# Sliding-window attention feeding a two-layer MLP on one core: one transpose instead of two for a unit's two key blocks, split again by masks

## The chip, the cores and the metric

The kernel runs on one NeuronCore of a Trainium2 chip, in one launch. The metric is the device time of a run in microseconds (us), as the median of its runs. Five engines matter: TensorE (PE in the profile, with its weight loads as PEld), VectorE (DVE), ScalarE (ACT), GpSimd (POOL) and SyncE (SP), which here issues every DMA. Each engine works through its own list of instructions in order; they meet through semaphores.

## What is computed

Four batches of eight heads of attention over 768 positions with head size 64, then a two-layer MLP over all 3072 tokens:

```python
scores = (q @ k.T) / sqrt(64)
keep   = (key < n_sink) | ((0 <= query - key) & (query - key < window))   # n_sink 4, window 128
a      = softmax(where(keep, scores, -1e9));  attn = a @ v
x      = attn with the heads side by side       # (4*768, 512)
r      = maximum(x @ w_in, 0)                   # w_in 512 x 2048
out    = (s * r * r + b) @ w_out                # w_out 2048 x 512
```

With a window of 128 a query block of 128 sees at most two key blocks: its own (keys not after the query) and the one before (keys less than 128 back). In the block before, the kept keys have a place in the block greater than the query's place; in its own block, not greater. The two kept triangles, laid on each other, don't overlap. The sink keys stand in 16 columns of their own.

## The kernel before, in words

The 3072 tokens are cut into eight chunks of 384 (three query blocks; two chunks a batch). Chunk 0 has a way of its own (`first_slots`), during which the MLP's weights are also loaded and converted. From then on `moe_steps` of chunk c is interleaved with `attn_slots` of chunk c+1. The MLP has 32 steps: for each of 16 slices of the hidden layer, L521 (12 matmuls, the first layer) and, two slices later, L540 (9 matmuls, the second). The last chunk's MLP has no attention beside it.

Precision is kept by splitting values in two: a rounded part (hi, type fp32r) and the rest (lo), which are multiplied apart.

An attention chunk has 24 units, one for each head and query block (h, i), and runs as a software pipeline, one slot at a time. In slot t it issues `unit_a` of unit t, `unit_b` of unit t-LB, `unit_c` of unit t-LC and `unit_d` of unit t-LC-LD; before the change LB, LC, LD are 2, 4, 1, so there are 29 slots, spread evenly over the 32 MLP steps.

- `unit_a`: two score matmuls (PE L293, L294), mask and row maximum (DVE L298), exponential with its row sum (ACT L304) into the tile `sm` (four buffers), and on POOL a copy of the sink columns into `psk` (L305).
- `unit_b`: one PE transpose for each key block of the exponentials: L316 for the block before, L317 for its own, both into the PSUM tile `tp`. Then hi is rounded out of `tp` by ACT (L321) and lo is what is left, by DVE (L322). The two parts go to `hl`. Where a unit has no block before it (first block of a sequence, in even chunks), there is no L316.
- `unit_c`: the value matmuls (PE L354) with `vv`, which hold hi and lo of the values; at the head's third block ACT (L362) and DVE (L363) gather the sum into `xm`; once a pair of heads, transposes of `psk` (L367) and two copies.
- `unit_d`: once a pair of heads, sink values and the scale 1/sum (L378, L380), two DVE operations on `xm` (L381, L382), then hi (ACT L383) and lo (POOL L384) of the MLP's input x.

Ahead of them `prep_head` splits queries (L268, L272), keys (ACT L271, POOL L273) and values (ACT L277, POOL L278), two slots before a head's first unit. SP issues the loads: queries L235, values L237, keys L250 (one raw buffer each), sink values L257.

The code is written against tiles. A scheduler orders the instructions of each engine ahead of time; the order of the program is their priority, and an instruction that opens a tile waits until a buffer of that tag is free. Nothing is reordered on the chip. PSUM has five buffers of tag `a` (scores, `tp`, the first layer's `h`, `o`, `os`, `zb`, `ts`) and three for the second layer's sums.

In the MLP, L521 gives `h`; ACT L524, DVE L526, ACT L528 and DVE L529 turn it into `g`, which L540 reads two slices later (three buffers of `g`).

Of the kernel before, what the change touches and what calls it, by code (L numbers as in the profile page):

```python
# [6 lines left out]
F32 = mybir.dt.float32  # L7
# [5 lines left out]
ALU = mybir.AluOpType  # L13
AX = mybir.AxisListType

P = 128
# [3 lines left out]
CH = BLK * P  # L20
# [6 lines left out]
MDT = mybir.dt.bfloat16  # L27
# [4 lines left out]
NARROW, NEARLY = 2, 8  # L32
RB, VB = 2, 2
E0, LB0, LC0 = 8, 4, 6
LB, LC, LD, L2 = 2, 4, 1, 2


@with_exitstack
def tile_kernel(ctx, tc, qT, kT, k0, v, vsk, n_sink, window, w, s, b, out):
    nc = tc.nc  # L40
# [21 lines left out]
    nw = const.tile([P, 2], F32, tag="nw", name="nw")  # L62
    n_ap, w_ap = nw[:, 0:1], nw[:, 1:2]
    W = 2 * P + NS
    msk = const.tile([P, 3 * W + P + NS], MDT, tag="msk", name="msk")
    m_1, m_odd, m_even = (msk[:, j * W:(j + 1) * W] for j in range(3))
    m_0 = msk[:, 3 * W:]
# [62 lines left out]
    def constants2():  # L130

        spread = wk.tile([P, P], F32, tag="y", name="spread", bufs=1)
        nc.gpsimd.memset(spread, 0.0)
        for j in range(2):
            nc.gpsimd.affine_select(
                out=spread[96:P].rearrange("p (a d) -> p a d", a=2), in_=spread[96:P].rearrange("p (a d) -> p a d", a=2),
                pattern=[[1, 2], [0, D]], compare_op=ALU.not_equal, fill=1.0, base=2 * j, channel_multiplier=-1)
        nc.scalar.copy(sel, spread)
        for t in psks:
            nc.gpsimd.memset(t, 0.0)  # L140

        nc.vector.tensor_tensor(out=tmp[:, :NS], in0=low[:, :NS], in1=snk[:, :NS], op=ALU.mult)
        nc.vector.tensor_tensor(out=tmp[:, :NS], in0=snk[:, :NS], in1=tmp[:, :NS], op=ALU.subtract)
        nc.vector.scalar_tensor_tensor(out=tm2[:, :NS], in0=rel1[:, :NS], scalar=w_ap, in1=snk[:, :NS],
                                       op0=ALU.is_ge, op1=ALU.mult)
        mask(m_0[:, :NS], tmp[:, :NS])
        mask(m_1[:, 2 * P:], tm2[:, :NS])
        mask(m_even[:, P:P + NS], snk[:, :NS])
        cp = nc.gpsimd.tensor_copy
        upm, lom = m_full[2][:, P:2 * P], m_full[2][:, 2 * P:]  # L150
        cp(out=m_0[:, NS:], in_=lom)
        for m, l0 in ((m_1, P), (m_even, P + NS), (m_odd, P)):
            cp(out=m[:, :P], in_=upm)
            cp(out=m[:, l0:l0 + P], in_=lom)
        cp(out=m_odd[:, 2 * P:], in_=m_even[:, P:P + NS])
# [125 lines left out]
    def unit_a(k, h, i):  # L281

        hd = k.heads[h]
        pp = k.pairs[h // 2]
        g = k.half * BLK + i
        u = (k.c * H + h) * BLK + i
        if k.half == 0:
            c0, n = ((0, 144), (16, 272), (144, 272))[i]
        else:
            c0, n = ((0, 272), (128, 272), (272, 272))[i]  # L290
        sc = ps("sc")
        qs = slice(i * P, (i + 1) * P)
        nc.tensor.matmul(sc[:, :n], hd.qs[:, qs], hd.kh[:, c0:c0 + n], start=True, stop=False)  # L293
        nc.tensor.matmul(sc[:, :n], hd.qs[:, qs], hd.kl[:, c0:c0 + n], start=False, stop=True)  # L294
        m = m_0 if g == 0 else m_1 if g == 1 else m_odd if g % 2 else m_even
        uu = slice(u, u + 1)
        sm = wk.tile([P, W], F32, name="sm", tag="sm", bufs=SMB)
        nc.vector.tensor_tensor_reduce(out=sm[:, :n], in0=sc[:, :n], in1=m, scale=-0.125, scalar=BIG,  # L298
                                       op0=ALU.add, op1=ALU.min, accum_out=negm[:, uu])

        k.cc[(h, i)] = (sm,) + ((NS, None, 0) if g == 0 else (P, 0, 2 * P) if g % 2 else (P + NS, 0, P))
        s0 = k.cc[(h, i)][3]
        hh = h % 2
        nc.scalar.activation(sm[:, :n], sm[:, :n], AF.Exp, bias=negm[:, uu], scale=-1.0, accum_out=pp.zz[:, i, hh:hh + 1])  # L304
        nc.gpsimd.tensor_copy(out=pp.psk[:, i, :6 * NS].rearrange("p (t x) -> p t x", t=3)[:, :, hh * NS:(hh + 1) * NS],  # L305
                              in_=sm[:, s0:s0 + NS].unsqueeze(1).to_broadcast([P, 3, NS]))

    def unit_b(k, h, i):

        sm, c0, p0, _ = k.cc.pop((h, i))  # L310
        hd = k.heads[h]
        if i == 0:
            hd.hl = wk.tile([P, 2, 2 * CH], F32R, name="hl", tag="hl", bufs=HLB)
        tp = ps("tp")
        if p0 is not None:
            nc.tensor.transpose(tp[:, :P], sm[:, p0:p0 + P], ident)  # L316
        nc.tensor.transpose(tp[:, P:2 * P], sm[:, c0:c0 + P], ident)  # L317

        a, z = (P if p0 is None else 0), 2 * P
        hi, lo = (hd.hl[:, t, i * z + a:(i + 1) * z] for t in range(2))  # L320
        nc.scalar.copy(hi, tp[:, a:z])  # L321
        nc.vector.tensor_tensor(out=lo, in0=tp[:, a:z], in1=hi.bitcast(F32), op=ALU.subtract)  # L322
        pp = k.pairs[h // 2]
        if h % 2 == 1 and i == BLK - 1:
            zr = wk.tile([P, 2, BLK, 2], F32, tag="zr", name="zr")
            zh = wk.tile([P, BLK, 2], F32R, tag="zh", name="zh")
            nc.vector.tensor_scalar(out=zr[:, 0], in0=pp.zz, scalar1=1e-9, scalar2=None, op0=ALU.add)
            nc.vector.reciprocal(out=zr[:, 1], in_=zr[:, 0])
            nc.vector.tensor_copy(zh, zr[:, 1])
            nc.gpsimd.tensor_copy(out=pp.psk[:, :, 96:98], in_=zh.bitcast(F32))  # L330
            nc.vector.tensor_tensor(out=pp.psk[:, :, 98:100], in0=zr[:, 1], in1=zh.bitcast(F32), op=ALU.subtract)

    def unit_c(k, h, i):

        hd = k.heads[h]
        pp = k.pairs[h // 2]
        cur = i if k.half == 0 else i + 1
        if i == 1:
            hd.o = ps("o")
            hd.n = 0  # L340

        mm = []
        if i == BLK - 1:
            mm.append((cur, 2 * i + 1, 1))
        if i > 0:
            mm.append((cur - 1, 2 * i - 1, 2))
        if i == 1 and k.half == 1:
            mm.append((0, 0, 1))  # L350
        for kb, c0, n in mm:
            for t in range(2):
                q0 = c0 // 2 * P
                nc.tensor.matmul(hd.o[:, q0:q0 + n * P], hd.vv[:, kb, :], hd.hl[:, t, c0 * P:(c0 + n) * P],  # L354
                                 start=(hd.n == 0), stop=(i == BLK - 1 and kb == cur - 1 and t == 1))
                hd.n += 1
        if i == BLK - 1:
            a, c = (0, D) if h % 2 == 0 else (D, 0)
            if h % 2 == 0:
                pp.x = wk.tile([P, CH], F32, tag="xm", name="xm")  # L360
                pp.y = wk.tile([P, CH], F32, tag="y", name="y", bufs=1)
            nc.scalar.copy(pp.y[a:a + D], hd.o[c:c + D, :CH])  # L362
            nc.vector.tensor_tensor(out=pp.x[a:a + D], in0=hd.o[a:a + D, :CH], in1=pp.y[a:a + D], op=ALU.add)  # L363
            if h % 2 == 1:
                ts = ps("ts")
                for j in range(BLK):
                    nc.tensor.transpose(ts[:, j * P:(j + 1) * P], pp.psk[:, j, :], ident)  # L367
                pp.xs = wk.tile([P, CH], F32R, tag="xsk", name="xsk", bufs=1)
                nc.scalar.copy(pp.xs, ts[:, :CH])
                nc.vector.tensor_tensor(out=pp.xs[32:64], in0=ts[32:64, :CH], in1=pp.xs[32:64].bitcast(F32), op=ALU.subtract)  # L370
# [15 lines left out]
    def attn_slots(c):  # L386
        k = new_chunk(c)
        units, ahead = [], {}
        for pr in range(H // 2):
            h, t0 = 2 * pr, 2 * BLK * pr  # L390
            units += [(h + hh, i) for hh in range(2) for i in range(BLK)]
            todo = ((-5, load_pair, pr), (-5, load_keys, h), (-2, load_sinks, pr), (-2, prep_head, h), (-2, load_keys, h + 1),
                    (1, prep_head, h + 1))
            for d, fn, a in todo:
                ahead.setdefault(max(t0 + d, 0), []).append((fn, a))
        n = len(units)

        def slot(t):
            def f():

                for fn, a in ahead.get(t, ()):
                    fn(k, a)
                if t < n:
                    unit_a(k, *units[t])
                if 0 <= t - LB < n:
                    unit_b(k, *units[t - LB])
                if 0 <= t - LC < n:
                    unit_c(k, *units[t - LC])
                if 0 <= t - LC - LD < n:
                    unit_d(k, *units[t - LC - LD])  # L410
            return f

        return k, [slot(t) for t in range(n + LC + LD)]


    def first_slots():
# [271 lines left out]
    for c in range(NC_):  # L688
# [4 lines left out]
        i = 0  # L693
# [57 lines left out]
```

## Time and profile before

| what | value |
|---|---|
| median of 3 runs | 783.11 us (782.27 to 783.18) |
| profiled execution, own time | 784.06 us |
| its span, first to last instruction | 782.2 us, so 1.9 us lie around it |
| mean granted TensorE clock | 0.983 |
| MLP of chunks 1, 3, 5 (attention of 2, 4, 6 beside it) | 86.47 us each |
| MLP of chunks 2, 4, 6 (attention of 3, 5, 7 beside it) | 89.40 to 89.43 us each |
| MLP of chunk 7, alone | 74.42 us |

How to read it: a row of the profile names the line of the code, the engine, what is written and read, the shape and the count. "Busy" is time in which the engine worked; matmuls overlap each other, so a matmul's duration is longer than the time that it takes from the next one, which is read from the distance between two starts. The time before the MLP of chunk 1 (to 180.09 us) holds the start-up, chunk 0, chunk 1's attention and the weights.

### The profile page before, as it was taken

Reading aid. Unit: us, or ns where it says so; the run is one execution under the profiler, and the core shown is the slowest. Engines: PE = TensorE matmul, PEld = TensorE weight load, DVE = VectorE, ACT = ScalarE, POOL = GpSimd, SP = SyncE. Lnnn points to the kernel's source line nnn. Section 1 sums busy time; section 2 is a strip of 40 time slices with the busy share of each in tenths; the row PEclk is TensorE's granted clock in tenths of the full one; section 3 lists DMA queues with packets and bytes.
Section 4 is the critical chain, followed back from the end, with each engine's and each line's share of the span. In section 5 each row is a group of like instructions: output and inputs, shape, how many; then the busy total and the mean of one; then the engine's idle time right before and its main releaser. Section 6 shows DMA issues by size and latency. Waiting matters only on the chain.

```text
span 782.2 us, 12150 instructions
## 1 busy us (share of the span) xinstructions
PE 736.0 (94%) x4036; PEld 656.5 (84%) x4036; DVE 510.5 (65%) x1251; ACT 495.0 (63%) x1231; POOL 263.4 (34%) x411
## 2 busy tenths in 40 slices
PE   6878887599999999999999999999999999999996
PEld 3656675489989999999989999999989999999985
DVE  5888899985676466665676466665676466653321
ACT  4896977766676576656676576656676576643222
POOL 3146567652333234232333234232333234210000
PEclk9998999989999999999999999999999999999999
DMA  7644304212111211112111211112111211001001
GB/s 275 268 148 176 111 14 160 85 34 75 43 44 53 85 47 52 49 43 76 43 43 53 86 47 53 49 43 76 43 43 53 85 47 53 28 1 41 1 1 44
DMA packets 28118, 54.21 MB, mean 69 GB/s; under 512 B 3600, under 2 KB 16528, under 8 KB 26128
## 3 DMA queue, kind: packets, MB, share of 16 engines
q1 hardware_dynamic: 28048, 53.36, 20.8%
q8 instruction: 34, 0.56, 0.3%
q14 instruction: 36, 0.29, 0.1%
HBM read 47.06 MB, written 6.29 MB: 68 GB/s over the span
## 4 chain that ended last, share of the span: by engine, by line
PE 77%; DVE 7%; ACT 6%; POOL 4%; issue 3%; DMA 1%; SPq 1%; POOLq 0%; DVEq 0%; ACTq 0%
PE h L521 31%; PE po L540 30%; PE o L354 5%; PE sc L294 2%; PE sc L293 2%; POOL w L203 2%; PE tp L317 2%; PE tp L316 2%; DVE w L201 1%; ACT w L199 1%; DVE wt L200 1%; PE o L480 1%; DMA sb<-in_s 1%; ACT sm L304 1%; ACT w L208 1%
## 5 line engine op out<-in xcount | busy, mean ns | idle before, releaser
L521 PE MATMUL h<-x,w 128*128 128x384 f32 x1536 | 301.1, 345 | 13.3 <-DVE r L526 7.2
L540 PE MATMUL po<-w,g 128*128 128x512 f32 x1152 | 298.5, 401 | 4.9 <-DVE g L529 3.7
L521 PEld LDWEIGHTS h<-x,w 128*128 128x128 f32 x1536 | 270.8, 191 | 21.4 <-issue 5.4
L540 PEld LDWEIGHTS po<-w,g 128*128 128x128 f32 x1152 | 209.4, 189 | 46.3 <-DVE g L529 5.5
L524 ACT ACTIVATE r<-h 128x384 f32<-128x384 f32 x128 | 62.8, 491 | 110.2 <-PE h L521 103.2
L298 DVE CUSTOM_DVE_ANT_0 sm<-sc,msk 128x272 f32<-128x272 f32 (+1 forms) x168 | 70.2, 418 | 82.4 <-PE sc L294 60.6
L529 DVE SCALAR_TENSOR_TENSOR g<-r,sb,g 128x384 fp32r<-128x384 f32 x128 | 87.2, 681 | 44.7 <-ACT g L528 42.6
L526 DVE SCALAR_TENSOR_TENSOR r<-h,sb,r 128x384 f32<-128x384 f32 x128 | 78.5, 613 | 52.7 <-ACT r L524 52.5
L305 POOL COPY psk<-sm 128x48 f32<-128x48 f32 x168 | 51.8, 309 | 168.4 <-ACT sm L304 167.3
L304 ACT ACTIVATE sm<-sm,negm 128x272 f32<-128x272 f32 (+1 forms) x168 | 85.3, 508 | 22.2 <-DVE negm L298 21.5
L528 ACT ACTIVATE g<-r,sb 128x384 fp32r<-128x384 f32 x128 | 78.8, 615 | 29.3 <-DVE r L526 29.0
L273 POOL TENSOR_TENSOR kl<-kraw,kh 128x544 fp32r<-128x544 f32 (+1 forms) x56 | 71.9, 1283 | 56.4 <-ACT kh L271 54.2
L321 ACT CAST hl<-tp 128x256 fp32r<-128x256 f32 (+1 forms) x168 | 59.1, 353 | 27.2 <-PE tp L317 26.6
L354 PE MATMUL o<-hl,vv 128*128 128x256 f32 (+1 forms) x400 | 71.6, 295 | 1.8 <-DVE hl L322 0.9
L322 DVE TENSOR_TENSOR hl<-tp,hl 128x256 fp32r<-128x256 f32 (+1 forms) x168 | 66.6, 398 | 8.0 <-ACT hl L321 6.1
L278 POOL TENSOR_TENSOR vv<-vraw,vv 128x256 fp32r<-128x256 f32 (+1 forms) x56 | 42.5, 758 | 60.7 <-ACT vv L277 58.7
L354 PEld LDWEIGHTS o<-hl,vv 128*128 128x128 f32 x400 | 55.0, 190 | 4.1 <-issue 1.4
L363 DVE TENSOR_TENSOR xm<-o,y 64x384 f32<-64x384 f32 x56 | 30.9, 552 | 31.5 <-ACT y L362 31.3
L294 PE MATMUL sc<-kl,qs 128*128 128x272 f32 (+1 forms) x168 | 48.7, 290 | 0.4 <-POOL kl L273 0.4
L293 PE MATMUL sc<-kh,qs 128*128 128x272 f32 (+1 forms) x168 | 47.9, 285 | 0.7 <-DVE qs L272 0.4
L272 DVE TENSOR_TENSOR qs<-qraw,qs 64x384 fp32r<-64x384 f32 x56 | 42.4, 758 | 6.2 <-ACT qs L268 4.5
L317 PE MATMUL tp<-identr,sm 128*128 128x128 f32 x168 | 46.0, 274 | 0.0
(113 smaller groups left out, 837.6 us busy)
## 6 DMA issues: line engine op xcount, KB each, us to landing
w<-in_w SPq DMA_DIRECT2D x15, 1024.0 KB, 10.0
kraw<-in_kT SPq DMA_DIRECT2D x32, 272.0 KB, 2.6
out<-ot SPq DMA_DIRECT2D x24, 256.0 KB, 2.0
qraw<-in_qT SPq DMA_DIRECT2D x28, 192.0 KB, 2.3
kraw<-in_kT SPq DMA_DIRECT2D x24, 208.0 KB, 2.4
vraw<-in_v SPq DMA_DIRECT2D x16, 256.0 KB, 2.6
vraw<-in_v SPq DMA_DIRECT2D x12, 192.0 KB, 2.3
vsraw<-in_vsk SPq DMA_DIRECT2D x28, 64.0 KB, 1.8
```

What stands on the lines that cost most here:

```text
L273: nc.gpsimd.tensor_tensor(out=hd.kl[:, :kw], in0=hd.k[:, :kw], in1=hd.kh[:, :kw].bitcast(F32), op=ALU.subtract)
L293: nc.tensor.matmul(sc[:, :n], hd.qs[:, qs], hd.kh[:, c0:c0 + n], start=True, stop=False)
L294: nc.tensor.matmul(sc[:, :n], hd.qs[:, qs], hd.kl[:, c0:c0 + n], start=False, stop=True)
L298: nc.vector.tensor_tensor_reduce(out=sm[:, :n], in0=sc[:, :n], in1=m, scale=-0.125, scalar=BIG, op0=ALU.add, op1=ALU.min, accum_out=negm[: ...
L304: nc.scalar.activation(sm[:, :n], sm[:, :n], AF.Exp, bias=negm[:, uu], scale=-1.0, accum_out=pp.zz[:, i, hh:hh + 1])
L322: nc.vector.tensor_tensor(out=lo, in0=tp[:, a:z], in1=hi.bitcast(F32), op=ALU.subtract)
L354: nc.tensor.matmul(hd.o[:, q0:q0 + n * P], hd.vv[:, kb, :], hd.hl[:, t, c0 * P:(c0 + n) * P], start=(hd.n == 0), stop=(i == BLK - 1 and kb ...
L521: nc.tensor.matmul(h[:, :CH], weight[f][:, 0, wi, cc * P:(cc + 1) * P], x[xi][:, cc, :], start=(i == 0), stop=(i == 11))
L526: nc.vector.scalar_tensor_tensor(out=r, in0=h[:, :CH], scalar=sw_ap, in1=r, op0=ALU.mult, op1=ALU.mult)
L528: nc.scalar.activation(gg[:, 0, :], r, AF.Identity, bias=b_ap, scale=1.0)
L529: nc.vector.scalar_tensor_tensor(out=gg[:, 1, :], in0=r, scalar=b_ap, in1=gg[:, 0, :].bitcast(F32), op0=ALU.add, op1=ALU.subtract)
L540: nc.tensor.matmul(po[tb], gg[:, gi, tsl], weight[f][:, 1, wi, :], start=(f == 0 and i == 0), stop=(f == NF - 1 and i == 2))
```

## The change

From the third attention chunk on (`k.c >= MERGED`, MERGED = 2), for every unit that has a block before it:

- right after the exponential, POOL adds the two key blocks of `sm`, 128x128 each, into the place of the unit's own block;
- `unit_b` transposes that sum alone (L316 is not issued);
- DVE multiplies the transposed sum by two masks (`split`, 128 x 2 x 128 in bf16, built once by two DVE operations in `constants2`) and writes a 128x256 tile `two` in SBUF, which has one buffer: first the block before, then the own block;
- ACT rounds hi out of `two` instead of `tp`, and lo is computed on POOL, from `two`, instead of on DVE from `tp`.

For these chunks LB goes from 2 to 3 and LC from 4 to 6, so that there are 31 slots. `xm` goes from two buffers to one. `sm` keeps its four buffers, and the values' `vv` its two.

```diff
-LB, LC, LD, L2 = 2, 4, 1, 2
+LB, LC, LD, L2 = (2, 3), (4, 6), 1, 2
+MERGED = 2
...
+    split = const.tile([P, 2, P], MDT, tag="split", name="split")
...
+        nc.vector.tensor_scalar(out=split[:, 0, :], in0=rel, scalar1=0.0, scalar2=None, op0=ALU.is_gt)
+        nc.vector.tensor_scalar(out=split[:, 1, :], in0=rel, scalar1=0.0, scalar2=None, op0=ALU.is_le)
...
+        if g > 0 and k.c >= MERGED:
+            c1, p1 = k.cc[(h, i)][1:3]
+            nc.gpsimd.tensor_tensor(out=sm[:, c1:c1 + P], in0=sm[:, p1:p1 + P], in1=sm[:, c1:c1 + P], op=ALU.add)
...
-        if p0 is not None:
+        merged = p0 is not None and k.c >= MERGED
+        if p0 is not None and not merged:
             nc.tensor.transpose(tp[:, :P], sm[:, p0:p0 + P], ident)
         nc.tensor.transpose(tp[:, P:2 * P], sm[:, c0:c0 + P], ident)
...
-        nc.scalar.copy(hi, tp[:, a:z])
-        nc.vector.tensor_tensor(out=lo, in0=tp[:, a:z], in1=hi.bitcast(F32), op=ALU.subtract)
+        if merged:
+            two = wk.tile([P, 2 * P], F32, tag="two", name="two", bufs=1)
+            nc.vector.tensor_tensor(out=two.rearrange("p (s c) -> p s c", s=2), in0=tp[:, P:2 * P].unsqueeze(1).to_broadcast([P, 2, P]),
+                                    in1=split, op=ALU.mult)
+            nc.scalar.copy(hi, two)
+            nc.gpsimd.tensor_tensor(out=lo, in0=two, in1=hi.bitcast(F32), op=ALU.subtract)
+        else:
+            nc.scalar.copy(hi, tp[:, a:z])
+            nc.vector.tensor_tensor(out=lo, in0=tp[:, a:z], in1=hi.bitcast(F32), op=ALU.subtract)
...
-                pp.x = wk.tile([P, CH], F32, tag="xm", name="xm")
+                pp.x = wk.tile([P, CH], F32, tag="xm", name="xm", bufs=1)
...
+        lb, lc = LB[c >= MERGED], LC[c >= MERGED]
...
-                if 0 <= t - LB < n:
-                    unit_b(k, *units[t - LB])
+                if 0 <= t - lb < n:
+                    unit_b(k, *units[t - lb])
...
-        return k, [slot(t) for t in range(n + LC + LD)]
+        return k, [slot(t) for t in range(n + lc + LD)]
```

(The calls of `unit_c` and `unit_d` take `lc` in the same way.)

## Rows read from the trace of the kernel before

**Rows 1.** The page's table of engines (busy us, share of the span, instructions), and the granted TensorE clock in 40 slices of the span, in tenths.
```profile
PE 736.0 (94%) x4036; PEld 656.5 (84%) x4036; DVE 510.5 (65%) x1251; ACT 495.0 (63%) x1231; POOL 263.4 (34%) x411
PEclk9998999989999999999999999999999999999999
```

**Rows 2.** Busy time of each engine by stretch. Each stretch runs from the first L521 matmul of one chunk's MLP to the next one's; columns: stretch, its length, busy us (and instructions) of each engine, granted clock, DMA share, GB/s. The first six are the MLPs of chunks 1 to 6 with the attention of chunks 2 to 7 beside them, the seventh is the MLP of chunk 7.
```profile
180.09:266.56 86.47, 85.98 (x493) 79.19 (x492) 55.39 (x148) 55.92 (x152) 28.11 (x53) 1.00 0.18 55
266.56:355.96 89.40, 89.08 (x517) 82.28 (x516) 57.64 (x148) 58.37 (x152) 29.38 (x53) 1.00 0.18 55
355.96:442.44 86.48, 85.99 (x493) 79.21 (x492) 55.40 (x148) 56.04 (x152) 27.75 (x53) 1.00 0.18 55
442.44:531.87 89.43, 89.11 (x518) 82.31 (x517) 57.58 (x148) 58.32 (x152) 29.39 (x53) 1.00 0.18 55
531.87:618.34 86.47, 85.98 (x493) 79.20 (x492) 55.36 (x148) 56.13 (x152) 27.76 (x53) 1.00 0.18 55
618.34:707.77 89.43, 89.11 (x518) 82.31 (x517) 57.06 (x150) 55.97 (x146) 25.37 (x49) 1.00 0.13 39
707.77:782.19 74.42, 67.90 (x339) 60.78 (x337) 19.94 (x33) 20.43 (x37) 0.89 (x1) 0.98 0.06 23
```

**Rows 3.** Timeline of PE, two places of the fifth attention chunk; columns: start us, duration us, what, count (instructions of one kind in a row are merged).
```profile
384.67 2.27 PE L540 MATMUL po<-w,g 128*128 128x512 f32 x9
386.78 0.29 PE L293 MATMUL sc<-kh,qs 128*128 128x272 f32 x1
...
395.39 0.29 PE L293 MATMUL sc<-kh,qs 128*128 128x272 f32 x1
395.51 0.29 PE L294 MATMUL sc<-kl,qs 128*128 128x272 f32 x1
395.64 0.27 PE L316 MATMUL tp<-identr,sm 128*128 128x128 f32 x1
395.75 0.27 PE L317 MATMUL tp<-identr,sm 128*128 128x128 f32 x1
395.78 2.35 PE L540 MATMUL po<-w,g 128*128 128x512 f32 x9
397.96 0.29 PE L293 MATMUL sc<-kh,qs 128*128 128x272 f32 x1
```

**Rows 4.** Groups of instructions by line and shape from 180 to 708 us: count, busy us, mean ns of one, idle time of the engine just before them and what ended it.
```profile
L316 PE MATMUL tp<-identr,sm 128*128 128x128 f32 x120 | 32.9, 274 | 0.0
L322 DVE TENSOR_TENSOR hl<-tp,hl 128x256 fp32r<-128x256 f32 x120 | 50.1, 417 | 7.6 <-ACT hl L321 6.1
L321 ACT CAST hl<-tp 128x256 fp32r<-128x256 f32 x120 | 44.3, 370 | 26.9 <-PE tp L317 26.4
L277 ACT CAST vv<-vraw 128x256 fp32r<-128x256 f32 x24 | 9.4, 393 | 0.0
L260 POOL TENSOR_TENSOR vs<-vsraw,vs 32x128 fp32r<-32x128 f32 x24 | 10.9, 455 | 53.6 <-issue 39.7 <-ACT vs L259 13.6
L278 POOL TENSOR_TENSOR vv<-vraw,vv 128x192 fp32r<-128x192 f32 x22 | 14.7, 667 | 29.7 <-ACT vv L277 29.3
L278 POOL TENSOR_TENSOR vv<-vraw,vv 128x256 fp32r<-128x256 f32 x24 | 18.1, 754 | 22.8 <-ACT vv L277 21.1
L305 POOL COPY psk<-sm 128x48 f32<-128x48 f32 x144 | 38.8, 269 | 161.2 <-ACT sm L304 160.3
L384 POOL TENSOR_TENSOR x<-xm,x 128x384 fp32r<-128x384 f32 x25 | 25.3, 1012 | 39.5 <-ACT x L383 39.5
L273 POOL TENSOR_TENSOR kl<-kraw,kh 128x544 fp32r<-128x544 f32 x24 | 32.6, 1357 | 29.2 <-ACT kh L271 28.0 <-PE tp L317 1.2
L273 POOL TENSOR_TENSOR kl<-kraw,kh 128x416 fp32r<-128x416 f32 x22 | 23.9, 1088 | 21.6 <-ACT kh L271 21.2 <-PE tp L317 0.3
```

**Rows 5.** The same view over the whole execution: the mask operations of the start-up on a 128x128 tile with a bf16 result.
```profile
L98 DVE TENSOR_SCALAR m_all<-sc 128x128 bf16<-128x128 f32 x6 | 0.9, 221 | 0.0
```

**Rows 6.** One line's instructions from 180 to 708 us: count, duration in ns (smallest, median, largest), first and last start, shape. L529 and L272 read two tiles in SBUF; L526 reads one in PSUM and one in SBUF.
```profile
L272 DVE TENSOR_TENSOR qs<-qraw,qs x46: 551/552/1031, 189.0 to 673.2; 64x384 fp32r<-64x384 f32 x46
L529 DVE SCALAR_TENSOR_TENSOR g<-r,sb,g x96: 599/619/687, 184.2 to 702.0; 128x384 fp32r<-128x384 f32 x96
L526 DVE SCALAR_TENSOR_TENSOR r<-h,sb,r x96: 601/614/621, 182.9 to 700.7; 128x384 f32<-128x384 f32 x96
L305 POOL COPY psk<-sm x144: 216/223/562, 183.5 to 693.9; 128x48 f32<-128x48 f32 x144
```

**Rows 7.** Timeline of ACT, DVE and POOL in the fourth attention chunk: start us, duration us, what; in brackets the engine's idle time before it and what ended that.
```profile
300.70 0.51 ACT L383 CAST x<-xm 128x384 fp32r<-128x384 f32 x1 [0.56 <-DVE xm L382]
301.30 1.01 POOL L384 TENSOR_TENSOR x<-xm,x 128x384 fp32r<-128x384 f32 x1 [0.79 <-ACT x L383]
...
303.17 0.35 ACT L321 CAST hl<-tp 128x256 fp32r<-128x256 f32 x1
303.55 0.42 DVE L322 TENSOR_TENSOR hl<-tp,hl 128x256 fp32r<-128x256 f32 x1
```

**Rows 8.** What SP's queue waited for, whole execution: us in total, times, longest us.
```profile
SPq L250 <- POOL kl L273: 168.8, 30, 14.9
SPq L237 <- POOL vv L278: 83.6, 23, 9.2
```

More of the change, by code (lines that the diff above doesn't have):

```diff
@@ L404, in f @@
                     unit_a(k, *units[t])
-                if 0 <= t - LB < n:
-                    unit_b(k, *units[t - LB])
[L407 to L410, printed above, removed]
+                if 0 <= t - lb < n:
+                    unit_b(k, *units[t - lb])
+                if 0 <= t - lc < n:
+                    unit_c(k, *units[t - lc])
+                if 0 <= t - lc - LD < n:
+                    unit_d(k, *units[t - lc - LD])
             return f
-        return k, [slot(t) for t in range(n + LC + LD)]
+        return k, [slot(t) for t in range(n + lc + LD)]
     def first_slots():
```

## The prediction

> **What bounds the kernel now.** I read the table of engines first. PE is busy for 736.0 of the 782.2 us of the span, DVE for 510.5, ACT for 495.0, POOL for only 263.4, and the granted clock is near full speed almost throughout [rows 1]. A share of the span is a mean over unlike stretches, so the second view is busy time by chunk. The reader is to see that from 180 us on PE leaves 0.49 us idle in a stretch of 86.47 us and 0.32 us in one of 89.40, at a granted clock of 1.00, while DVE and ACT each idle for about 31 us and POOL for about 60 [rows 2]. The six stretches are the ones in which attention chunks 2 to 7 run, just those that the change touches. Here time is what PE has to issue, and an instruction taken from PE is worth what it takes of PE's sequence.
>
> That is not its duration, since matmuls overlap. The third view, PE's timeline, gives the distances: a score matmul starts at 395.39, the first transpose at 395.64, the second at 395.75, so the first takes 0.11 us [rows 3]. A second way: from 395.39 to the next unit's score matmul at 397.96 are 2.57 us, with nine L540 in them, and nine L540 alone take 386.78 - 384.67 = 2.11; of the remaining 0.46 the two score matmuls take 395.64 - 395.39 = 0.25, which leaves 0.21 for two transposes, 0.105 each [rows 3]. The 274 ns of the group's row [rows 4] would be two and a half times too much.
>
> **The change part by part.**
> PE, removed: chunks 3, 5, 7 have 24 units with a block before, chunks 2, 4, 6 have 16, so 3 x 24 + 3 x 16 = 120 of L316, which is the count of the row [rows 4]. Between 0.105 and 0.11 I take 0.108: 120 x 0.108 = 13.0 us (12.6 to 13.2), 2.6 for an odd attention chunk and 1.7 for an even one. No PE work is added. The transpose that stays reads the sum instead of one block: the same shape, the same time.
>
> POOL, added: an add of 128 elements a partition and a subtract of 256. The subtract has its row, 754 ns at 256 elements; the add lies between 455 ns (128 elements on 32 partitions) and 667 (192 elements on 128), and I take the first, since that is its length in each partition [rows 4]. Together 1.21 us a unit, 29.0 for an odd chunk and 19.3 for an even one, which brings POOL from 29.4 to 58.4 us of 86.8, and from 28 to 47 of 84.8 [rows 2]. It stays beside PE, at nothing, as long as its queue keeps pace.
>
> DVE: the subtract (417 ns, one PSUM and one SBUF input) goes, a multiply of the same shape with one PSUM and one SBUF input comes; I take 417 for it too [rows 4], so nothing. Its bf16 mask, and the PSUM tile read twice, have no row; I bound it by 221 ns, the operation with a bf16 tile on 128 columns [rows 5], and 614, L526 on 384 [rows 6]: 24 units x 0.2 make 5 us a chunk either way, against 31 idle. ACT: the copy reads SBUF, 393 ns instead of 370 [rows 4], 24 x 0.023 = 0.6 us a chunk, hidden by ACT's 31 idle us. If these covers were gone, the two would cost at most their own 5.6 us a chunk.
>
> Start-up: two mask operations at 221 ns [rows 5], 0.4 us on DVE before 180 us, where PE does wait for others; I take all 0.4, bounds 0 and 0.4.
>
> The new order in the queues. Before, DVE waited for ACT; now ACT waits for DVE, POOL for ACT, and, because `two` has one buffer, the next unit's DVE multiply for POOL's subtract. Behind that multiply in DVE's list stand L298, L526 and L529, and PE's next scores, `h` buffers and second layer wait for those. The loop is 0.42 + 0.39 + 0.75 [rows 4] plus three handoffs of 0.03 to 0.09 [rows 7], 1.75 us, and a slot of an odd chunk has 86.8 / 31 = 2.80. About 1.05 us is left for what stands ahead in ACT's and POOL's lists. A key split of 1357 ns comes once a head, so one unit in three [rows 4]. It can overrun by 0.3 alone, by 0.8 with an ACT operation of 0.5 ahead too; DVE has a third of its time idle to catch up. The POOL add stands in front of the transpose, but units now wait three slots instead of two, 8.4 us, for the chain mask, exponential, add.
>
> SP: no DMA is added or moved. But the values' buffers come free at slot +8 after a head's first unit instead of +6 (`unit_c` moved), so the POOL split of the next values, and the load L237 that waits for it (83.6 us of waits), come about two slots later, with key loads L250 behind it in the same list; L250 itself already waits 168.8 us for POOL's key splits [rows 8]. Keys are split two slots, 5.6 us, ahead of their scores; that hides it, and I cost it at nothing. Without that cover each of 48 heads would wait for a key split, up to 1.36 us, which makes 65 us; I keep to nothing, since the values that came late are themselves used only seven slots after a head's first scores, and leave the other end outside the range with the worst of the cases below. `xm` with one buffer: L384, 1.01 us [rows 4], reads it last, two slots before the next pair writes; nothing.
>
> Stalls that PE gets from all this: none is the lower end. PE idles 3 x 0.49 + 3 x 0.32 = 2.4 us in the six stretches today [rows 2]. With POOL's load doubled I take another 2 us.
>
> DVE and POOL in each other's way: L272 takes 552 ns in the median and up to 1031, POOL's sink copy 223 and up to 562; L526, with one input in PSUM, never leaves 601 to 621 [rows 6]. With POOL twice as busy, 16 L529 and 8 L272 a chunk may each be held for part of a 0.75 us subtract, at most 24 x 0.75 = 18 us on DVE, whose 58 would become 76 of 86.8: still not the bound. The Trainium skill (SBUF — State Buffer, "Who interferes with whom") has the same rule: a VectorE instruction with two SBUF inputs and a GpSimd one that reads SBUF keep each other out for a whole instruction, one with a single SBUF input does not. By it the moved subtract meets L529 and L272, and the new multiply meets nothing; the sum would stay, and case (a) below gains weight.
>
> **The sum.** Against the profiled execution: 784.06 - 13.0 + 0.4 + 2.0 = 773.5. The median of the runs is 0.95 lower than that execution, so 772.5 as a median, 1.4% less.
>
> **The rivals.**
> (a) *Part of the gain goes into the loop around `two`.* For: the loop's 1.75 us with a key split and an ACT operation ahead is 3.6 against 2.8. If nothing hid the overrun, 8 heads x 0.8 = 6.4 us an odd chunk and, with a split of 1.09 on shorter keys [rows 4], about 5 an even one: 34 us. Against: DVE's 31 idle us and the second layer's two slices of lead hide most. A quarter coming through is 8.5: 784.06 - 13.0 + 0.4 + 8.5 - 0.95 = 779.
> (b) *Slower: POOL becomes the pace.* Its list is in order. Today it waits 160.3 us for the exponentials before 144 sink copies, 1.11 each [rows 4], at no cost. If it kept all these waits, 24 x 1.11 = 26.7 in a chunk, and waited for ACT's copy before each subtract too (0.48, 11.6), an odd chunk would take 58.4 + 26.7 + 11.6 = 96.7, 7.3 over today's 89.4, while an even one with 47.2 + 26.7 + 7.7 = 81.6 stays under PE. 784.06 + 3 x 7.3 - 3 x 1.7 + 0.4 - 0.95 = 800. It decides from 89.4 - 58.4 = 31.0 us of waits on, 1.29 a unit. For: two more in-order waits on one engine, and a single buffer that hands its delay to DVE. Against: a POOL that lags finds its inputs ready, so the waits shrink just when it gets late; the three slots between stages let it lag.
> (c) *The change does nothing on PE.* Excluded by the count: 120 matmuls and weight loads are not issued, and PE's stretches have no idle time in which they could have been free.
>
> **How the numbers follow.** A measurement of this kernel tells about 0.2% (1.6 us) from no change. Forecast 0.62; (a) 0.18, of which 0.13 ends faster and 0.05 within 0.2%; (b) 0.20. I give (b) that much because the order of the lists was fixed ahead of time and I can't see it. So faster 0.75, same 0.05, slower 0.20. The forecast's own range is 769 (13.2 saved, no stall, part of today's idle time gone) to 776; the range goes on through (a) and the first part of (b), to 786.
>
> **What would show it.** Right: L316 falls from 144 to 24; the six stretches shorten by about 2.4 and 1.5 us with PE still under 1 us idle in each; POOL rises to about 58 and 47 us, L322's group to 48 with the multiply at about 417 ns beside it; `sm`'s sum and the subtract near 0.46 and 0.75. Wrong: PE idle of several us in a stretch, ended by DVE L298, L526 or L529, or by POOL's add ahead of the transpose; DVE's multiply waiting for POOL's subtract; odd chunks that lose more than even ones, as (b) says; new operations well over their rows.

## The result and the profile after

The changed kernel takes 792.26 us (median of 4 runs, 791.73 to 792.89) against 783.14 for the kernel before beside it: a ratio of 1.0112, interval 1.0098 to 1.0125. It is slower by 1.1%; forecast was 772.5, in a range of 769 to 786.

The span of the profiled execution is 790.2 us, 8.0 more than before. Busy time by chunk, cut as in [rows 2] at the first L537 matmul of each chunk's MLP (lines have shifted: L537 is the old L521, L556 the old L540):

```profile
178.94:267.29 88.35, 84.77 (x478) 77.47 (x476) 58.23 (x148) 56.30 (x152) 47.45 (x85) 1.00 0.18 54
267.29:358.21 90.92, 86.95 (x493) 79.60 (x492) 62.93 (x148) 58.76 (x152) 58.33 (x101) 1.00 0.18 54
358.21:446.57 88.36, 84.78 (x477) 77.44 (x476) 58.30 (x148) 56.37 (x152) 46.97 (x85) 1.00 0.18 54
446.57:537.51 90.94, 87.03 (x494) 79.65 (x492) 62.68 (x148) 58.49 (x152) 58.40 (x101) 1.00 0.18 54
537.51:625.86 88.35, 84.75 (x477) 77.44 (x476) 58.40 (x148) 56.33 (x152) 46.96 (x85) 1.00 0.18 54
625.86:715.60 89.74, 86.97 (x494) 79.60 (x493) 60.15 (x150) 56.63 (x146) 54.56 (x97) 1.00 0.13 39
```

The six stretches last 536.66 us against 527.68 [rows 2]. PE is busy for 515.25 of them instead of 525.25, so the work did leave PE; but it idles for 21.4 us instead of 2.4. POOL stands at 47 and 58 us, as worked out, and has over 31 us idle in every stretch. The granted clock is 1.00 as before. The first stretch begins 1.15 us earlier than before, so the start-up lost nothing.

Who ended PE's idle time, from the view of waits between 179 and 716 us (engine, line, by whom; us in total, times, longest), and two waits of the new path:

```profile
PE os L393 <- DVE xsk L385: 21.4, 18, 1.3
POOL hl L334 <- ACT hl L333: 18.3, 34, 1.9
DVE two L331 <- POOL hl L334: 2.6, 11, 0.3
```

The one wait of PE is that of the sink values' matmul `os` (`unit_d`) for DVE's last step on the sink tile `xsk` (`unit_c`, one slot earlier). It comes 18 times, at three of the four pairs of each chunk; 17 of the waits last 1.2 to 1.3 us, the last one 0.2. Before, the same wait held 2.4 us in six times. The loop around `two`, of which I had feared most, is 2.6 us.

The groups of the new path, 179 to 716 us, to be held against [rows 4], and the query split L276, the old L272, whose row before is in [rows 6]:

```profile
L331 DVE TENSOR_TENSOR two<-tp,split 128x256 f32<-128x256 f32 x120 | 50.2, 418 | 16.4 <-PE tp L325 12.9 <-POOL hl L334 2.6
L333 ACT CAST hl<-two 128x256 fp32r<-128x256 f32 x120 | 47.4, 395 | 5.5 <-DVE two L331 4.7
L334 POOL TENSOR_TENSOR hl<-two,hl 128x256 fp32r<-128x256 f32 x120 | 97.9, 816 | 19.2 <-ACT hl L333 18.3 <-PE po L556 0.3 <-DMA kraw<-in_kT 0.2
L311 POOL TENSOR_TENSOR sm<-sm 128x128 f32<-128x128 f32 x120 | 58.7, 489 | 83.4 <-ACT sm L308 76.0 <-DMA qraw<-in_qT 5.1
...
L276 DVE TENSOR_TENSOR qs<-qraw,qs 64x384 fp32r<-64x384 f32 x46 | 43.7, 950 | 5.4 <-ACT qs L272 4.3
```

The multiply takes 418 ns (417 forecast), the copy 395 (393), the add 489 (455), the subtract 816 (754). None of them is the surprise.

One of the 18 places, first PE's timeline, then DVE's (start us, duration us, what; in brackets the idle time before it):

```profile
586.29 0.49 PE L382 MATMUL ts<-identr,psk 128*128 128x128 f32 x3
586.53 2.36 PE L537 MATMUL h<-x,w 128*128 128x384 f32 x12
588.73 0.23 PE L297 MATMUL sc<-kh,qs 128*128 128x144 f32 x1
588.79 0.28 PE L298 MATMUL sc<-kl,qs 128*128 128x144 f32 x1
588.90 0.29 PE L325 MATMUL tp<-identr,sm 128*128 128x128 f32 x1
590.41 0.45 PE L393 MATMUL os<-xsk,vs 128*128 128x384 f32 x1 [1.21 <-DVE xsk L385]
```

```profile
586.28 0.42 DVE L331 TENSOR_TENSOR two<-tp,split 128x256 f32<-128x256 f32 x1
586.90 1.01 DVE L276 TENSOR_TENSOR qs<-qraw,qs 64x384 fp32r<-64x384 f32 x1 [0.20 <-ACT qs L272]
587.94 0.32 DVE L342 TENSOR_SCALAR zr<-zz 128x6 f32<-128x6 f32 x1
588.29 0.19 DVE L343 RECIPROCAL zr<-zr 128x6 f32<-128x6 f32 x1
588.52 0.46 DVE L344 CAST zh<-zr 128x6 fp32r<-128x6 f32 x1
589.01 0.17 DVE L346 TENSOR_TENSOR psk<-zr,zh 128x6 f32<-128x6 f32 x1
589.21 0.56 DVE L378 TENSOR_TENSOR xm<-o,y 64x384 f32<-64x384 f32 x1
589.80 0.55 DVE L385 TENSOR_TENSOR xsk<-ts,xsk 32x384 fp32r<-32x384 f32 x1
```

PE transposes the sink tile (`ts`) and has one step of the MLP, 2.2 us, and a unit's scores and transpose to do before it needs the result. In that time DVE, without a pause after 586.90, works through a query split that takes 1.01 us instead of 0.55, four small operations on the sums of the *next* pair of heads (L342 to L346, 1.24 us from the first's start to the last's end), `xm`, and only then `xsk`. The sums are traced in `unit_b`, but the scheduler put them where their input is ready, at the exponential of the next pair's last unit. That unit runs `unit_a` in slot 6p + 11, for pair p; with values six units behind, pair p's last `unit_c` falls into the same slot 6p + 11. With four it fell into 6p + 9.

DVE's list is not the whole of the 1.21 us. What `xm` and `xsk` read from ACT was ready here:

```profile
588.08 0.47 ACT L377 COPY y<-o 64x384 f32<-64x384 f32 x1
588.58 0.48 ACT L384 CAST xsk<-ts 128x384 fp32r<-128x384 f32 x1
```

With nothing else in front of them the two DVE operations could have started at 588.58 and ended at about 589.72 instead of 590.35 (an estimate from these rows). So about 0.6 us of the wait is DVE's list, and the rest would have stayed for ACT's copies.

From this came two theories: S, the place of the work (six units are just a pair's length, so two pairs' work meets in one slot ahead of PE's sink matmul), and W, the added work itself (POOL's operations and its hold on DVE, that is, DVE operations that last longer while POOL works).

### The profile page after: what moved, and what is told of

Same layout as the page of the kernel before. It is cut to its first block, busy times and chain, and to the rows that moved or that the text cites. A ratio compares the mean times of both kernels' runs of the same rounds, so it can differ in the third digit from the quotient of the medians.

```text
span 790.2 us, 12333 instructions
## 1 busy us (share of the span) xinstructions
PE 726.6 (92%) x3916; PEld 643.7 (81%) x3916; DVE 533.1 (67%) x1253; ACT 497.4 (63%) x1231; POOL 408.3 (52%) x651
## 4 chain that ended last, share of the span: by engine, by line
PE 73%; DVE 10%; ACT 6%; POOL 4%; issue 4%; DMA 1%; SPq 1%; POOLq 0%; DVEq 0%; ACTq 0%
PE po L556 30%; PE h L537 28%; PE o L369 5%; PE sc L298 2%; PE sc L297 2%; PE tp L325 2%; POOL w L207 2%; DVE qs L276 2%; DVE xsk L385 1%; DVE w L205 1%; ACT w L203 1%; PE os L393 1%; DVE wt L204 1%; DVE xm L378 1%; DMA sb<-in_s 1%
## 5 line engine op out<-in xcount | busy, mean ns | idle before, releaser
L537 PE MATMUL h<-x,w 128*128 128x384 f32 x1536 | 303.2, 346 | 12.4 <-DVE r L542 6.6
L556 PE MATMUL po<-w,g 128*128 128x512 f32 x1152 | 300.4, 401 | 4.5 <-DVE g L545 3.5
L537 PEld LDWEIGHTS h<-x,w 128*128 128x128 f32 x1536 | 270.7, 191 | 20.8 <-ACT w L212 4.9
L556 PEld LDWEIGHTS po<-w,g 128*128 128x128 f32 x1152 | 210.1, 189 | 45.2 <-DVE g L545 4.8
L545 DVE SCALAR_TENSOR_TENSOR g<-r,sb,g 128x384 fp32r<-128x384 f32 x128 | 97.8, 764 | 40.7 <-ACT g L544 38.1
L540 ACT ACTIVATE r<-h 128x384 f32<-128x384 f32 x128 | 62.9, 491 | 95.0 <-PE h L537 90.2
L542 DVE SCALAR_TENSOR_TENSOR r<-h,sb,r 128x384 f32<-128x384 f32 x128 | 78.6, 614 | 49.2 <-ACT r L540 48.7
L334 POOL TENSOR_TENSOR hl<-two,hl 128x256 fp32r<-128x256 f32 x120 | 97.9, 816 | 19.2 <-ACT hl L333 18.3
L311 POOL TENSOR_TENSOR sm<-sm 128x128 f32<-128x128 f32 x120 | 58.7, 489 | 83.4 <-ACT sm L308 76.0
L282 POOL TENSOR_TENSOR vv<-vraw,vv 128x256 fp32r<-128x256 f32 (+1 forms) x56 | 44.4, 793 | 39.7 <-ACT vv L281 39.6
L276 DVE TENSOR_TENSOR qs<-qraw,qs 64x384 fp32r<-64x384 f32 x56 | 57.2, 1021 | 6.6 <-ACT qs L272 5.3
L331 DVE TENSOR_TENSOR two<-tp,split 128x256 f32<-128x256 f32 x120 | 50.2, 418 | 16.4 <-PE tp L325 12.9
L399 POOL TENSOR_TENSOR x<-xm,x 128x384 fp32r<-128x384 f32 x28 | 29.6, 1059 | 50.4 <-ACT x L398 50.4
L207 POOL TENSOR_TENSOR w<-w 128x1024 int32<-128x1024 int32 (+1 forms) x17 | 32.4, 1908 | 36.0 <-DVE z L474 19.4
L333 ACT CAST hl<-two 128x256 fp32r<-128x256 f32 x120 | 47.4, 395 | 5.5 <-DVE two L331 4.7
```

The source lines that it names most:

```text
L276: nc.vector.tensor_tensor(out=hd.qs[other], in0=hd.q, in1=hd.qs[hd.half].bitcast(F32), op=ALU.subtract)
L334: nc.gpsimd.tensor_tensor(out=lo, in0=two, in1=hi.bitcast(F32), op=ALU.subtract)
L537: nc.tensor.matmul(h[:, :CH], weight[f][:, 0, wi, cc * P:(cc + 1) * P], x[xi][:, cc, :], start=(i == 0), stop=(i == 11))
L540: nc.scalar.activation(r, h[:, :CH], AF.Relu, scale=1.0 / WUP)
L542: nc.vector.scalar_tensor_tensor(out=r, in0=h[:, :CH], scalar=sw_ap, in1=r, op0=ALU.mult, op1=ALU.mult)
L545: nc.vector.scalar_tensor_tensor(out=gg[:, 1, :], in0=r, scalar=b_ap, in1=gg[:, 0, :].bitcast(F32), op0=ALU.add, op1=ALU.subtract)
```

## Experiments

Each run is timed beside the kernel before, on the same chip; a ratio is to that one. "Waits" are PE's between 179 and 720 us.

**One slot more for the sink chain.**
```diff
-LB, LC, LD, L2 = (2, 3), (4, 6), 1, 2
+LB, LC, LD, L2 = (2, 3), (4, 6), (1, 2), 2
```


> The changed kernel, with unit_d two slots behind unit_c instead of one in the chunks of the change. Theory S (sink chain): the time was lost where PE's sink matmul waits for DVE's last step on the sink tile, one slot behind, 18 waits of 1.2 to 1.3 us, 22 us in all; with a slot more they go and the 13 us of the transposes show: 770 to 776 us. Rival W (added work): the new GpSimd work and its lock on DVE make DVE and ACT late whatever waits for them; PE then waits in other places: 785 to 792 us.

783.55 us, ratio 1.000 (0.999 to 1.0009). Between the two. The wait at `os`, 21.4 us, is gone, yet the time falls by 8.7 only, since PE now waits 8.4 us, 12 times, before L537 for DVE's score operation (which frees a PSUM buffer), and 2.8 us for POOL at the chunk's end. At all 12 places the sums, `xm` and `xsk` stand in DVE's list ahead of that operation. The late DVE list shows in another place: theory S had named too narrow a place, theory W is not excluded.

**Depth alone: nothing merged, three and six units behind.**
```diff
-LB, LC, LD, L2 = 2, 4, 1, 2
+LB, LC, LD, L2 = (2, 3), (4, 6), 1, 2
+MERGED = 2
...
```


> The kernel before, with nothing merged, but its stages three and six units behind from the third chunk on, as in the change. Theory S: the sixth unit puts the sink chain of a pair into the slot in which the next pair's sums and the queries of the one after are made, so the waits before the sink matmul arise here too, somewhat shorter as GpSimd is not in the way: 787 to 793 us. Rival W: depth alone costs nothing: 782 to 785 us.

796.62 us, ratio 1.0173 (1.0156 to 1.019): worse than forecast by S, and slower than the changed kernel. The distances alone lose more than the whole change lost; the merged path on top of them gains. DVE's timeline at one of the places, then the two splits on POOL beside it, and the wait:

```profile
588.99 0.42 DVE L323 TENSOR_TENSOR hl<-tp,hl 128x256 fp32r<-128x256 f32 x1 [0.16 <-ACT hl L322]
589.52 0.36 DVE L328 TENSOR_SCALAR zr<-zz 128x6 f32<-128x6 f32 x1
589.91 0.19 DVE L329 RECIPROCAL zr<-zr 128x6 f32<-128x6 f32 x1
590.14 0.46 DVE L330 CAST zh<-zr 128x6 fp32r<-128x6 f32 x1
590.63 0.17 DVE L332 TENSOR_TENSOR psk<-zr,zh 128x6 f32<-128x6 f32 x1
590.83 0.56 DVE L364 TENSOR_TENSOR xm<-o,y 64x384 f32<-64x384 f32 x1
591.42 0.55 DVE L371 TENSOR_TENSOR xsk<-ts,xsk 32x384 fp32r<-32x384 f32 x1
592.00 0.56 DVE L273 TENSOR_TENSOR qs<-qraw,qs 64x384 fp32r<-64x384 f32 x1
```
```profile
588.77 1.08 POOL L274 TENSOR_TENSOR kl<-kraw,kh 128x416 fp32r<-128x416 f32 x1 [1.82 <-ACT kh L272]
589.97 0.60 POOL L279 TENSOR_TENSOR vv<-vraw,vv 128x192 fp32r<-128x192 f32 x1
```
```profile
PE os L379 <- DVE xsk L371: 11.3, 18, 0.9
```

The same sums stand ahead of `xsk`, with no POOL work added; here the query split comes after it and takes 0.56. But POOL's old work lengthens the sums too: L328 takes 0.36 and ends 0.03 us after the key split, L330 takes 0.46 and ends 0.03 us after the value split, where 0.17 is the shortest of either. So this run shows that the waits come without the added work, not that they come without POOL's hold. PE's idle time in the six stretches is 8.9 us over before; the profiled span is 11.5 us longer, and the rest was not traced to a wait.

**Depth of five, nothing merged** (the same edit with (4, 5)).

> The kernel before with nothing merged, its stages three and five units behind from the third chunk on: the depth-only run with one unit less. Theory S (it is the meeting of two pairs' work in one slot that costs, and only six units, a pair's length, bring it about): 781 to 785 us. Rival D (every unit of depth costs): half of the depth-only run's 13 us, 788 to 791 us.

783.74 us, ratio 1.0005 (0.9995 to 1.0014), and `os` waits 2.2 us in all, as before. Depth is free up to five units; the sixth costs 13 us. So it isn't depth as such but which slots meet.

**The merged path with the old distances** ((2, 2), (4, 4) in the changed kernel).

> The changed kernel with the old distances, two and four units behind. Theory S: no long waits before the sink matmul, the transposes are saved: 771 to 776 us. Rival W: the added work makes it late with less room than the changed kernel had: 788 to 800 us.

781.01 us, ratio 0.9973 (0.9963 to 0.9984): between the two forecasts. Even attention chunks take 84.8 to 84.9 us, 1.6 less than before, about what their 16 transposes are worth; odd ones 90.3, 90.7 and 89.5, as long as before or longer [rows 2], with `os` waiting 7.4 us in all, up to 1.4 each. No sums stand in front there; the added work comes late in the fuller chunks with two slots, which is W's part. At the longest waits L545 in front takes 0.96 us, against 0.62 in the median of the changed kernel. What makes it late was not tested.

**Values five units behind** ((2, 3), (4, 5) in the changed kernel).

> The changed kernel with values five units behind instead of six. Theory S: the sink chain comes one slot ahead of the next pair's sums; waits before the sink matmul shorter than 0.6 us: 772 to 780 us. Rival W: like the changed kernel, 789 to 794 us.

774.58 us, ratio 0.9889 (0.9873 to 0.9906), as S had it. One number makes the change a gain of 1.1%; `os` waits 3.1 us, up to 0.7.

**The sums queued behind.** All distances as in the change, with one order on DVE (`k.sunk` is the last sink operation, `xsk`, of the pair before):
```diff
+            with tc.issue_after(k.sunk.ins) if k.c >= MERGED and h > 1 else nullcontext():
+                nc.vector.tensor_scalar(out=zr[:, 0], in0=pp.zz, scalar1=1e-9, scalar2=None, op0=ALU.add)
...
```


> The changed kernel, with one order given by hand on DVE: the five small operations on a pair's sums are queued behind the last sink operation of the pair before. Nothing else moves. Theory S1 (the sums stand ahead of the sink operation because of the sixth unit): the waits before the sink matmul shrink by the sums' 1.0 us, from 1.2 to 0.2 or 0.3 us: 774 to 780 us. Rival S2 (what makes the sink operation late is GpSimd holding DVE's query split, 0.46 us, and other DVE work that has come in front): the waits stay over 0.7 us: 784 to 790 us.

780.31 us, ratio 0.9965 (0.9952 to 0.9978): 12 us less than the changed kernel for the place of four small operations of a pair (the fifth of the block runs on POOL, on what the others make).

```profile
PE os L395 <- DVE xsk L387: 9.0, 18, 0.6
```
```profile
576.88 0.42 DVE L332 TENSOR_TENSOR two<-tp,split 128x256 f32<-128x256 f32 x1
577.49 1.00 DVE L277 TENSOR_TENSOR qs<-qraw,qs 64x384 fp32r<-64x384 f32 x1 [0.19 <-ACT qs L273]
579.18 0.56 DVE L380 TENSOR_TENSOR xm<-o,y 64x384 f32<-64x384 f32 x1 [0.69 <-ACT y L379]
579.77 0.55 DVE L387 TENSOR_TENSOR xsk<-ts,xsk 32x384 fp32r<-32x384 f32 x1
580.35 0.17 DVE L344 TENSOR_SCALAR zr<-zz 128x6 f32<-128x6 f32 x1
```

The sums now follow `xsk`. At 17 of the 18 places 0.4 to 0.6 us of PE's wait are left, and at each of these DVE waits 0.4 to 0.7 us for ACT's copy L379 (0.69 at the one shown) although the query split takes 1.0 to 1.3 us: what is left is ACT's lateness, as estimated above. ACT works without a pause there from the key split on, through the query split, the exponential, the value split and L334, to L379. My forecast of 774 to 780 was narrowly missed for that reason.

**The next pair's splits a slot earlier**, on top of that (`prep_head` of a pair's first head three slots ahead).

> The run with the sums queued behind (780.3 us), and the next pair's first queries and keys split three slots ahead instead of two, so not in the slot of the sink tile. Theory S: what is left of the waits before the sink matmul, 0.45 to 0.58 us each, comes from those splits on ACT and DVE and goes: 773 to 777 us. Rival: it comes from the merged path itself (multiply, copy): 779 to 782 us.

779.25 us, ratio 0.9954 (0.9937 to 0.9971). Inconclusive: in the trace the splits of queries and keys still stand in the same slot and order, so the edit didn't move what it was to move, and the wait is 8.8 us.

**Dead POOL work on the depth-only run.**
```diff
+            nc.gpsimd.tensor_tensor(out=scr[:, :P], in0=sm[:, p1:p1 + P], in1=sm[:, c1:c1 + P], op=ALU.add)
...
+            nc.gpsimd.tensor_tensor(out=scr, in0=hi.bitcast(F32), in1=hi.bitcast(F32), op=ALU.subtract)
```


> The kernel of the depth-only run (nothing merged, two transposes, 796.6 us) with the two GpSimd operations of the change added as dead work: an add of 128 and a subtract of 256 elements for each merged unit, into a scratch tile that nobody reads; one buffer for xm as in the change. Theory L (GpSimd's presence holds DVE's two-input operations): the query split rises to about 1.0 us as in the changed kernel and the waits before the sink matmul from 0.6 to about 1.0 us: 801 to 806 us. Rival M (it is the new dependences of the merged path that made the other half): 796 to 799 us.

788.27 us, ratio 1.0065 (1.0048 to 1.0082): less than the 796.62 without the dead work, which neither theory forecast. `os` waits 4.0 us instead of 11.3. The query split stays at 0.55 us. The lists of PE, DVE and ACT have the same order in both runs, over the whole execution; only POOL's differs. What changed on DVE is how long the first and the third of the sums take, in the depth-only run and then here (179 to 720 us):

```profile
L328 DVE TENSOR_SCALAR zr<-zz 128x6 f32<-128x6 f32 x24 | 12.3, 512 | 2.2
L330 DVE CAST zh<-zr 128x6 fp32r<-128x6 f32 x24 | 10.7, 446 | 0.8
```
```profile
L334 DVE TENSOR_SCALAR zr<-zz 128x6 f32<-128x6 f32 x24 | 11.5, 477 | 2.7 <-ACT sm L306 1.3
L336 DVE CAST zh<-zr 128x6 fp32r<-128x6 f32 x24 | 4.2, 176 | 0.8
PE os L385 <- DVE xsk L377: 4.0, 11, 0.6
```

The two take 7.3 us less in all, and `os` waits 7.3 us less. In the depth-only run POOL's value split ran beside L330; here the dead operations come before that split, and the conversion is through when it starts. So theory L had the right mechanism on the wrong operation and with the wrong sign: POOL's hold on operations ahead of `xsk` sets much of the price of the sixth unit, and dead work lowered it by moving POOL's value split.

**The sink tile one unit earlier** (its transposes and two copies at the pair's second to last unit):
```diff
-            if h % 2 == 1:
+        if h % 2 == 1 and i == (BLK - 2 if k.c >= MERGED else BLK - 1):
                 ts = ps("ts")
                 ...
```


> The changed kernel, with the transposes of the sink tile and its two copies issued one unit earlier (at the pair's second to last unit instead of the last), all distances as in the change. Theory S: the sink matmul finds its tile ready, its waits go, and 13 us of transposes less one microsecond of other waits show: 771 to 776 us. Rival W (added work makes PE late in other places as well): 781 to 790 us.

781.48 us, ratio 0.9976 (0.9966 to 0.9985), in W's range. `os` no longer waits; what waits is the matmul behind it, for the PSUM buffer that the gathering L378 frees, itself behind the same sums on DVE:

```profile
PE zb L395 <- DVE xm L378: 11.3, 12, 1.1
```

**Both: sink tile earlier, sums behind the last gathering (the L378 of the run before).**

> The run with the sink tile made one unit earlier (781.5 us), and the sums queued on DVE behind the last gathering of the pair before. Theory S: the waits that had come in place of the old ones (the second sink matmul, for a PSUM buffer that this gathering frees, 11 us) are the same late DVE list and go with the sums: 772 to 776 us. Rival: they stay, being due to the merged path: 779 to 783 us.

771.38 us, ratio 0.9845 (0.9828 to 0.9861), with all distances of the change and all its added work. Busy time by chunk:

```profile
179.27:264.35 85.08, 84.78 (x477) 77.46 (x476) 58.29 (x148) 56.14 (x152) 47.76 (x85) 1.00 0.19 56
264.35:351.48 87.13, 86.61 (x494) 79.52 (x493) 62.77 (x148) 58.80 (x152) 58.43 (x101) 1.00 0.19 56
351.48:436.25 84.77, 84.48 (x478) 77.39 (x476) 57.77 (x148) 56.14 (x152) 47.36 (x85) 1.00 0.19 56
436.25:523.37 87.12, 86.59 (x493) 79.53 (x492) 62.28 (x148) 58.61 (x152) 58.47 (x101) 1.00 0.19 56
```

PE idles 0.3 and 0.5 us a stretch again, with POOL at 47 and 58 us and DVE at 58 and 62, within 1 us of the changed kernel. Against the changed kernel the same work on the same engines is 20.9 us apart, by the place of the sink tile and of the sums alone.

**Five units with the sink tile earlier**, and **the same with the sums behind**:

> The changed kernel with values five units behind and the sink tile made one unit earlier. Theory S: the last waits before the sink matmul (3 us in all with five units) go as well: 771 to 773.5 us, faster than five units alone (774.6). Rival: no better than that, 774 to 777 us.

773.60 us, ratio 0.9874 (0.9856 to 0.9893): between the two ranges, and not told apart from five units alone.

> Five units, sink tile one unit earlier (773.6 us), and the sums queued behind the last gathering of the pair before. With five units the two don't meet, so theory S expects no change: 772 to 775 us. Were the sums costly wherever they stand, 770 to 772 us.

772.78 us, ratio 0.9866 (0.9849 to 0.9882): as S has it, the sums matter little where they don't meet the sink chain.

## Why the prediction was wrong, step by step

- *PE, removed*: right. 13.0 us were forecast for 120 transposes; the run with both repairs is 12.1 us under the kernel before beside it (783.49 - 771.38), its even chunks 1.4 to 1.7 and odd ones 2.3 us shorter than [rows 2] (1.7 and 2.6 forecast). That is the whole change with its order mended; no run took out the transposes alone.
- *POOL, DVE and ACT, added*: right in size (58.4 and 47 us on POOL forecast, 58.3 and 47 found; 418, 395, 489 and 816 ns), and right that it hides: all of it is there in the 771.38.
- *Start-up*: 0.4 us was taken, nothing was lost.
- **The step that failed** is "The new order in the queues", with the stalls put at 2 us. They are 19.0 us over before in the profiled execution, 21.4 in all, and in a place that the step didn't name. I went through the distances for what each wait gives a single unit more room (three slots before the transpose, seven before the values, two for `xm`), and none of these shows among PE's waits. I didn't lay pairs against each other: that a pair's `unit_c` moves by two slots into the slot where the next pair's last exponential ends, and that work of one pair which is ready there, the sums, goes ahead of the other's on DVE, one slot before PE needs it. The balance of the six stretches: PE idle +19.0, PE busy -10.0, sum +9.0 (536.66 - 527.68); with both repairs busy falls by 11.7, so some 1.7 us of what the transposes gave seems to be lost around the waits as well (an estimate from busy times).
- *Rival (a), the loop around `two`*: the mechanism is there and small, 2.6 us of DVE's waiting, none of PE's in its name.
- *Rival (b), POOL as the pace*: right in sign alone. Nothing in PE's waits ends with POOL. Odd chunks lost less than even ones (1.5, 1.5 and 0.3 against 1.9 us), where (b) wanted them to lose all. Its threshold, 31.0 us of POOL's waits in an odd chunk, was passed (90.92 - 58.33 = 32.6) without being a cause: an engine that is idle because its inputs come slowly is no pacemaker.
- *DVE and POOL in each other's way*: real and within the size taken for DVE's busy time (3 to 5 us more in a chunk, of 18 at most), but wrongly priced at nothing for PE. DVE's share of a stretch was the wrong measure: PE waited on one chain in DVE's list, and the hold lengthens that chain. The query split's mean went from 630 to 950 ns (552 to 916 in the median), while L542, the old L526 with one input in PSUM, kept its mean (615, before 613). The Trainium skill's rule (SBUF — State Buffer, "Who interferes with whom") agrees with that; it leaves room, too, for the hold on the small sums, which the prediction's words on it left out: conversions and operations of L342's kind can, where their operands allow it, run in a mode with two ports and then contend, though each has one input in SBUF. No view here shows the mode. In the place shown, 0.46 us is the split's 1.01 against 0.55, with POOL's key split running at that time, and 0.44 the two sums' 0.32 and 0.46 against 0.17 each. How the changed kernel's loss divides between the hold and the sums' own time was not tested there. In the kernel with depth alone it was: 7.3 of its 11.3 us of `os` waits go when the sums are held less. The run with both repairs shows that the split can take 914 ns in the median without costing PE anything.

What stays open: that division in the changed kernel, and which of the splits ahead of it makes ACT's copy late in the 9 us that are left with the sums behind.

## What to carry to other kernels

A pipeline distance must be read against the length of the groups that share work at their ends: when the distance equals that length, the late stage of one group's last unit and the early stage of the next group's last unit land in the same slot, and what is ready first can go ahead of what is needed first. Before a distance is moved, list each engine's instructions in the slot that holds the once-a-group work, and see who waits for the last of them; if one must be late, give the order by hand. On such a chain count each operation with what the neighbouring engine adds to it. When a change that takes work from the bound gains nothing, look for PE's one long wait: here the cure was an order, not less work.

## What the runs showed of the hardware that was not expected

A 128x6 operation on DVE, L342, took 0.32 us at the place shown and 0.17 at the place shown of the run with the sums behind (L344 there); the conversion after it took 0.46. In the changed kernel POOL was at work beside them, and each of the two ended about 0.03 us after a POOL instruction did (588.26 after 588.23, 588.98 after 588.95). It is no accident of the place: in the kernel before, the changed kernel and the two depth runs with six units, all 125 executions of these two operations that took more than 0.22 us (179 to 720 us) ended 0.025 to 0.034 us after a POOL instruction, mostly a key or value split. So small operations with one input in SBUF were held too, and on a chain they are worth their mean from the stretch in question, not their smallest duration. And a busy share does not tell whether an engine is the reason for PE's idle time: in the second stretch DVE worked 62.9 us in the changed kernel, where PE idled 4.0 us and waited for it, and 62.8 in the run with both repairs, where PE idled 0.5.
